# Reordering the start-up round of a fused RWKV-6 and MLP kernel: table load, row sums and two idle products

## The chip, the cores and the metric

The kernel runs on one core of a Trainium2 chip. The metric is the device time of one execution in microseconds (us), lower is better. Every run reported here gave the correct result. An execution is called fast when it is no more than 1.5% above the fastest of its kernel. All were, but for two: one of 22 executions of end_only, at 591.47 us (1.51% above), counts as slow and is left out of what follows, and one kernel was executed once, so its state is unknown. Here TensorE does the matrix products and transposes, VectorE, ScalarE and GpSimd work element by element, and SyncE issues most transfers (255 of 260 in the trace of the kernel before, ScalarE the other five).

## The reference

Two stages in fp32, with B=4, H=8, S=768, D=48, d_model=384, d_ff=1536:

```python
state = zeros(B, H, D, D)
for t in range(S):                                   # rwkv6_finch
    cur = einsum("bhd,bhe->bhde", u * k[t], v[t])
    y[t] = einsum("bhd,bhde->bhe", r[t], state + cur)
    state = w[t][..., None] * state + einsum("bhd,bhe->bhde", k[t], v[t])
x = y, heads side by side                            # (B, S, 384)
xn = (x - mean) / sqrt(var + 1e-6) * g_ln            # metaformer MLP
out = x + relu(xn @ w_ch1) @ w_ch2
```

## The kernel before

The work is cut into eight rounds, each of two units of four heads. A round transposes w, r and k, builds the lower triangle of the attention matrix in levels 0 to 5 (`quads` makes the products a_ps on TensorE, `grow` multiplies r and k by partial products of w on VectorE, `keep` puts the masked part into A), and forms states, outputs y and the MLP (h_ps, o_ps). The term of u needs only row sums of r·u·k: `product_sums`, called own_ps in the profile. Later rounds hide their attention under the MLP of the round before. Round 0 has no MLP to hide under, and all of the change lies there.

```python
def warm(n, tag="m"):              # idle products: only meant to keep TensorE's clock up
    while n > 0:
        m = min(n, RN // P)        # RN // P = 3, P = 128
        ps = (ps_m if tag == "m" else ps_t).tile([P, RN], F32, tag=tag, name="idle")
        PE.matmul(ps[:, 0 : m * P], nought.broadcast_to([P, P]),
                  nought.broadcast_to([P, m * P]), start=True, stop=True)
        n -= m

def product_sums(q):               # twelve products of TWO columns each
    ...
    for pr in pairs:
        for c in range(TT):
            PE.matmul(ps[:, ts(pr * TT + c, 2)], a["ruk"][pr][:, ts(c, P)],
                      sel[:, NP * g + pr], start=True, stop=True)
    ...
    ACT.copy(out=o.rearrange("p c (r j) -> p r c j", j=2),
             in_=ps[:, 0 : 2 * NK].rearrange("p (r c j) -> p r c j", r=NP, j=2))

def quads(q, lev):                 # 48 small products for one unit
    ...
    for c in range(NK):
        for i in range(2):
            for j in range(2):
                m = 2 * c + i
                rows = ds(HP * j, D)
                PE.matmul(a_ps[rnd][ds(C * (i ^ j), C), j, uu, c]...,
                          K[rows, ts(m, C)], R[rows, m, :, 1, :], start=True, stop=True)
```

The middle of round 0 (`run(ahead...)` makes six transposes for the next round; `begin` starts the load and conversion of a piece of the MLP's weights):

```python
for lev in range(1, NLEV):
    quads(u0, lev)
    quads(u1, lev)
    run(ahead[2 * lev - 2 : 2 * lev] if lev < NLEV - 1 else [])
    if lev in (2, 3, 4):
        begin()
    if lev == 1:
        product_sums(u0)
    elif lev < NLEV - 1:
        warm(3)
    for which in ("rk",) if lev < NLEV - 1 else "kr":
        for q in (u0, u1):
            grow(q, lev, which)
    keep(0, lev)
```

## Time and profile before

| | before |
|---|---|
| median of the first three runs | 587.24 us (587.1 to 587.42) |
| span of the profiled execution | 583.9 us |
| TensorE busy | 98% of the span |
| mean granted TensorE clock | 0.991 of full |

Two lines of the page of the kernel before also belong here. The first gives each engine's busy time, share and number of instructions (PE is TensorE, PEld its weight loads). The second gives, for one DMA queue, packets, megabytes and share of the sixteen DMA engines' time:

```profile
PE 572.2 (98%) x8558; PEld 384.1 (66%) x8558; DVE 273.6 (47%) x576; ACT 193.8 (33%) x423; POOL 90.6 (16%) x124
...
q8 instruction: 67, 1.10, 0.8%
```

TensorE executes 8558 products and as many weight loads, 17,116 instructions. Queue 8 carries 67 packets of 16.4 KB. Divided, that is 255 instructions for a packet, or 257 with the 92 waits of TensorE's sequencer. My estimate from these counts is that TensorE's program reaches it over this queue, in blocks of 256; shift64 below tests it. Over 584 us that is nothing, but in the levels of round 0 TensorE needs about 208 instructions in 2.9 us. The rate is the point there, not the share.

The chain of waits of the kernel before through levels 3, 4 and 5 of round 0 (start, length, what):

```profile
25.58 2.72 PE a_ps L49 x96
...
30.85 1.53 PE a_ps L49 x96
...
33.84 1.53 PE a_ps L49 x96
```

The products of level 3 run at half clock (2.72 in place of 1.53; the granted clock is 0.50 from 23.70 to 30.53), those of levels 4 and 5 at full clock. These three starts are what the change was to bring forward.

### The profile page before, as it was taken

How to read it: one execution, taken by the hardware profiler on the slowest of the kernel's cores; microseconds unless marked ns; L12 is line 12 of the kernel's file. 1: busy time of each engine (PE TensorE's matmuls, PEld its weight loads, DVE VectorE, ACT ScalarE, POOL GpSimd, SP SyncE). 2: the span in 40 equal slices, each digit the busy share in tenths (PEclk: the TensorE clock that was granted, in tenths of full speed). 3: DMA queues.
4: the chain of work that ended last, by engine and by line, in shares of the span. 5: the costliest groups of instructions: out<-in, count | busy, mean ns of one | idle time of the engine just before them, and what ended most of it. 6: DMA issues, size and time to landing. Idle time of an engine off the chain costs nothing.

```text
span 583.9 us, 19053 instructions
## 1 busy us (share of the span) xinstructions
PE 572.2 (98%) x8558; PEld 384.1 (66%) x8558; DVE 273.6 (47%) x576; ACT 193.8 (33%) x423; POOL 90.6 (16%) x124
## 2 busy tenths in 40 slices
PE   9999989999999999999999999999999999999997
PEld 7876756666666766666766666666666666666554
DVE  4879898687273634343452543336254531130000
ACT  3577686313442234311432125312331015202200
POOL 6140011104440035000620007000320000000000
PEclk9899899999999999999999999999999999999999
DMA  9938684036315311340204302031000000000000
GB/s 230 203 102 178 175 239 117 16 78 137 64 22 102 72 36 21 68 92 15 57 8 89 65 29 43 2 64 28 15 2 2 16 28 2 2 15 27 0 15 27
DMA packets 114192, 36.52 MB, mean 63 GB/s; under 512 B 104768, under 2 KB 111040, under 8 KB 114112
## 3 DMA queue, kind: packets, MB, share of 16 engines
q1 hardware_dynamic: 112240, 34.72, 26.5%
q8 instruction: 67, 1.10, 0.8%
q10 hardware_dynamic: 1872, 0.59, 0.4%
q14 instruction: 13, 0.11, 0.1%
HBM read 28.51 MB, written 4.72 MB: 57 GB/s over the span
## 4 chain that ended last, share of the span: by engine, by line
PE 91%; ACT 4%; DVE 2%; issue 1%; DMA 1%; ACTq 0%; DVEq 0%
PE o_ps L49 32%; PE h_ps L49 30%; PE a_ps L49 11%; PE y L49 4%; PE kv L49 2%; PE k_ps L49 2%; PE r_ps L49 2%; PE w_ps L49 2%; PE kn_ps L49 2%; PE xT_ps L49 1%; ACT rest L49 1%; PE own_ps L49 1%; PE idle L49 1%; ACT rkT L49 1%; ACT w_sb L49 1%
## 5 line engine op out<-in xcount | busy, mean ns | idle before, releaser
L49 PE MATMUL o_ps<-w_sb,h 128*128 128x384 f32 x576 | 199.0, 490 | 0.9 <-ACT h L49 0.9
L49 PE MATMUL h_ps<-xT,w_sb 128*128 128x384 f32 x576 | 198.7, 493 | 0.0
L49 PEld LDWEIGHTS h_ps<-xT,w_sb 128*128 128x128 f32 x576 | 105.7, 191 | 63.1 <-issue 0.9
L49 PEld LDWEIGHTS o_ps<-w_sb,h 128*128 128x128 f32 x576 | 104.4, 190 | 62.0 <-ACT h L49 1.8
L49 DVE TENSOR_TENSOR rkT<-rkT,tot 128x768 f32<-128x768 f32 (+1 forms) x96 | 76.7, 841 | 38.9 <-issue 26.0
L49 ACT ACTIVATE h<-h_ps 128x384 f32<-128x384 f32 x96 | 46.8, 488 | 144.7 <-PE h_ps L49 144.6
L49 PEld LDWEIGHTS a_ps<-rkT 48*64 48x64 f32 x4608 | 73.2, 136 | 20.8 <-issue 13.4
L49 PE MATMUL a_ps<-rkT 48*64 48x32 f32 x4608 | 78.4, 221 | 0.1
L49 DVE TENSOR_TENSOR o<-o_ps,x 128x384 f32<-128x384 f32 x24 | 13.4, 557 | 121.9 <-PE o_ps L49 121.8
L49 POOL TENSOR_TENSOR vo<-v,own 128x576 f32<-128x576 f32 x16 | 19.2, 1203 | 288.7 <-DVE own L49 251.9
L49 DVE SCALAR_TENSOR_TENSOR s<-s,decay,kv 128x48 f32<-128x48 f32 x160 | 29.3, 259 | 33.9 <-PE kv L49 33.9
L49 DVE TENSOR_TENSOR x<-y,vo 128x288 f32<-128x288 f32 x32 | 13.2, 453 | 53.8 <-PE y L49 53.7
L49 DVE COPY_PREDICATED A<-mask,a_ps 128x768 f32<-128x768 int8 x32 | 38.3, 1197 | 0.0
L49 ACT COPY rkT<-k_ps 128x384 f32<-128x384 f32 x31 | 13.9, 478 | 57.3 <-PE k_ps L49 57.1
L49 ACT ACTIVATE xT<-xT_ps,g_sb 128x384 f32<-128x384 f32 x24 | 13.6, 579 | 54.0 <-PE xT_ps L49 54.0
L49 ACT COPY rkT<-r_ps 128x384 f32<-128x384 f32 x31 | 14.2, 478 | 24.2 <-PE r_ps L49 24.1
L49 DVE TENSOR_SCALAR w_sb<-w_sb 128x384 f32<-128x384 f32 (+1 forms) x48 | 19.5, 406 | 0.8
L49 ACT ACTIVATE rstd<-mv,eps 128x3 f32<-128x3 f32 x8 | 2.4, 296 | 49.2 <-DVE mv L49 49.1
L49 DVE TENSOR_REDUCE own<-rk 128x12 f32<-128x576 f32 x12 | 9.0, 750 | 20.7 <-POOL rk L49 20.6
L49 ACT COPY wT<-w_ps 128x384 f32<-128x384 f32 x31 | 14.0, 478 | 14.1 <-PE w_ps L49 14.1
L49 PE MATMUL r_ps<-ident,nat_r 128*128 128x128 f32 x108 | 16.2, 279 | 2.2 <-ACT rkT L49 2.1
L49 DVE TENSOR_TENSOR rkT<-rkT,wT 128x768 f32<-128x768 f32 x16 | 17.5, 1131 | 0.9 <-PE a_ps L49 0.8
(76 smaller groups left out, 517.9 us busy)
## 6 DMA issues: line engine op xcount, KB each, us to landing
raw<-in_moe_w_ch_dram SPq DMA_DIRECT2D x24, 384.0 KB, 4.3
v<-in_v_dram SPq DMA_DIRECT2D x48, 96.0 KB, 3.3
out_dram<-o SPq DMA_DIRECT2D x24, 192.0 KB, 1.9
nat_w<-in_w_dram SPq DMA_DIRECT2D x42, 96.0 KB, 2.9
nat_r<-in_r_dram SPq DMA_DIRECT2D x42, 96.0 KB, 2.8
nat_k<-in_k_dram SPq DMA_DIRECT2D x42, 96.0 KB, 3.1
vx<-v SPq DMA_DIRECT2D x28, 72.0 KB, 2.3
nat_r<-in_r_dram ACTq DMA_DIRECT2D x2, 288.0 KB, 4.9
```

The lines of the kernel that those rows point to most:

```text
L49: return lambda *args, **kw: self.tc.keep_in_program_order(f(*args, **kw))
```

## The change

It has four parts. (1) **Table**: ScalarE loads its function table and takes its first root while nat_r is still in flight; the load of r of unit 1 goes later, and the load of g_sb goes to SyncE. (2) **Sums**: in level 1 the row sums of unit 0 go between the two halves of the products. (3) **Idle in level 1**: the idle product, so far in levels 2 to 4, is added there. (4) **End**: an idle product of three pieces before the outputs of unit 0 becomes one of two pieces before the outputs of unit 1.

```diff
--- before.py
+++ after.py
@@ -155,10 +155,17 @@
             )
 
 
+    nought = const.tile([P, 1], F32, name="nought")
+    DVE.memset(nought, 0.0)
+    eps = const.tile([P, 1], F32, name="eps")
+    DVE.memset(eps, 1e-6)
+    load_rows("r", 0, ACT)
+
+    ACT.activation(out=const.tile([P, 1], F32, name="root"), in_=eps, func=AF.Sqrt)
     for q in range(U):
         load_rows("w", q, SPO)
-        load_rows("r", q, ACT)
         load_rows("k", q, SPO)
+    load_rows("r", 1, ACT)
 
     sel = const.tile([P, H // 2, 2], F32, name="sel")
     POOL.memset(sel, 0.0)
@@ -167,16 +174,9 @@
             out=sel[ds(HP * j, D), :, j], in_=u.rearrange("(r j) d -> j d r", j=2)[j]
         )
     g_sb = const.tile([P, KC], F32, name="g_sb")
-    ACT.dma_start(out=g_sb, in_=moe_g_ln.rearrange("(kc p) -> p kc", p=P))
     u_bc = const.tile([P, H, D], F32, name="u_bc")
     ident = const.tile([P, P], F32, name="ident")
     make_identity(nc, ident)
-    nought = const.tile([P, 1], F32, name="nought")
-    DVE.memset(nought, 0.0)
-    eps = const.tile([P, 1], F32, name="eps")
-    DVE.memset(eps, 1e-6)
-
-    ACT.activation(out=const.tile([P, 1], F32, name="root"), in_=eps, func=AF.Sqrt)
     for q in range(U):
         for nm in "wrk":
             POOL.memset(flat(nm, q)[:, NH * TT * D :], 0.0)
@@ -752,19 +752,20 @@
     begin()
     begin()
     load(new[1], "k", SPO)
+    SPO.dma_start(out=g_sb, in_=moe_g_ln.rearrange("(kc p) -> p kc", p=P))
     warm(3)
     grow(u1, 0)
     keep(0, 0)
     ahead = each(turned, new[:1], "wrk", pairs) + each(turned, new[1:], "wrk", pairs)
     for lev in range(1, NLEV):
         quads(u0, lev)
+        if lev == 1:
+            product_sums(u0)
         quads(u1, lev)
         run(ahead[2 * lev - 2 : 2 * lev] if lev < NLEV - 1 else [])
         if lev in (2, 3, 4):
             begin()
-        if lev == 1:
-            product_sums(u0)
-        elif lev < NLEV - 1:
+        if lev < NLEV - 1:
             warm(3)
         for which in ("rk",) if lev < NLEV - 1 else "kr":
             for q in (u0, u1):
@@ -786,12 +787,12 @@
     product_sums(u1)
     own_term(u1, POOL)
     own_outputs(u0)
-    warm(3, "t")
     outputs(u0)
     exchanged(u1)
     begin()
     shifted()
     own_outputs(u1, "m")
+    warm(2, "t")
     outputs(u1)
     moments(0)
     load(units_of(2)[0], "w", SPO)
```

## The prediction

> **What bounds the kernel now.** I read the page first, then the chain of waits, then the timeline of single engines, then busy time and granted clock by stretch. The page says where a gain could lie at all:
>
> ```profile
> PE   9999989999999999999999999999999999999997
> PEclk9899899999999999999999999999999999999999
> PE 91%; ACT 4%; DVE 2%; issue 1%; DMA 1%; ACTq 0%; DVEq 0%
> ```
>
> TensorE is full in nearly all of the 40 slices of 14.6 us; all four parts of the change lie in the first 46 us of 583.9. The only slices where the granted clock falls below 9 tenths are the second and the fifth. So the change can save only what delays TensorE in the first three or four slices. Whatever is saved there is handed on, because the later rounds are an unbroken row of products.
>
> The chain of waits of the start (start, length, what):
>
> ```profile
> 0.80 4.04 DMA nat_r<-in_r_dram
> 4.86 0.39 ACTq L49
> 5.28 1.28 ACT L49
> 6.58 0.20 ACT root L49
> 6.78 0.38 ACT wT L49
> 7.20 1.53 PE r_ps L49 x12
> ```
>
> ScalarE issues its fifth transfer (g_sb) only when nat_r has landed (4.84), because that transfer reuses nat_r's completion semaphore; then come the function table (1.28), the root, and only then the copy that frees the bank for the transposes of r.
>
> The timeline of TensorE in level 1 and 2 of round 0 (start, length, product, count):
>
> ```profile
> 17.42 1.73 PE L49 MATMUL a_ps<-rkT 48*64 48x32 f32 x96
> 20.20 1.50 PE L49 MATMUL own_ps<-sel,ruk 128*128 128x2 f32 x12 [0.24 <-ACT wT L49]
> 24.09 1.49 PE L49 MATMUL idle<-nought 128*128 128x384 f32 x2
> 25.51 2.79 PE L49 MATMUL a_ps<-rkT 48*64 48x32 f32 x96
> ```
>
> The same 96 products take 1.73 us and then 2.79 us. Stretches of 3.41 us, TensorE alone, show why (stretch, length, busy and count, granted clock, DMA):
>
> ```profile
> 20.29:23.70 3.41, 3.41 (x113) 1.00 0.67 114
> 23.70:27.12 3.42, 3.42 (x66) 0.50 0.93 209
> 27.12:30.53 3.41, 3.41 (x53) 0.50 1.06 239
> 37.36:40.77 3.41, 3.41 (x137) 1.00 0.17 62
> 57.84:61.25 3.41, 3.41 (x94) 1.00 0.74 186
> 61.25:64.66 3.41, 3.41 (x9) 0.50 0.75 190
> ```
>
> The clock is halved from 23.70 to 30.53 and from 61.25 to 64.66. Every stretch before such a fall holds the sums (own_ps), 0.12 us each for two columns: TensorE counts as busy throughout, the array does almost nothing.
>
> [...] the edges 6.64, 23.70, 30.53, 61.25, 64.66 differ by 5, 2, 9 and 1 windows of 3.413. (Before 6.64 the page has no record and shows 1.00, but transposes start 0.213 us apart against 0.109 later, so it was half.) [...]
>
> To see what a window needs I estimate array work: a product of 384 columns on the whole array is two passes of 0.32 us (six passes take 1.94). Scaled by rows, columns and length, 96 pieces of a_ps make 0.48 us, six transposes 0.64, an idle product 0.64, twelve sums 0.02. The lowest shares of a window are then 0.10 (57.84, fell), 0.28 (20.29, fell), 0.36 (37.36, held). So a fall needs less than about 0.32. Cold windows with 0.61 and 0.64 stayed cold, 0.77, 0.82 and 0.84 became warm.
>
> **The change, part by part.**
>
> *Table first.* Table and root now run during nat_r's flight, at about 1.4 to 2.9. The second transfer of sel inherits the wait for nat_r (4.86 to about 5.4), in front of the first copy. w_ps_0 ends at 6.13, so that copy starts near 6.17, not 6.69. But the second half of w_ps, at half clock, ends at 7.10 anyway, and VectorE's copy of it runs 7.14 to 7.70: r_ps_0 can start at 6.94 instead of 7.20, r_ps_1 only at 7.75 instead of 7.91. A stall between groups costs one matmul's restart (0.06), and the chain then goes through VectorE's copies: 0.10 us remains of 0.52. nat_r of unit 1 leaves 1.6 us later, but its transposes come at 12.5: no cost. g_sb goes to SyncE and is used at 49.7: none.
>
> *Sums between the units.* Twelve sums, 1.42 us, move from behind w_ps to between the two halves (0.77 each) of the level's products. The 0.24 wait for a bank goes. The second half ends at about 20.3 instead of 19.0, so VectorE's second product of level 1 and its mask copy (1.87) end near 23.25 instead of 22.58.
>
> *Idle product in level 1.* Adds 0.75 (0.74 to 0.84 in the four warm cases). TensorE then reaches level 2 at 21.75 instead of 21.62, so the two parts cost 0.13 of TensorE in themselves. Their purpose is the clock. If no window fell, levels of 2.9 us (products 1.53, transposes 0.65, idle 0.75; VectorE needs 2.9 too) would bring level 5 to 30.65 instead of 33.77: 3.1 us saved.
>
> I don't believe all of that. With the window edges where this trace has them, 16.88 to 20.29 now holds the idle product, 96 pieces and the sums, but no longer the transposes: (0.32 + 0.48) / 3.41 = 0.24, which falls. The next, cold, holds transposes 1.28, idle 1.28 and some pieces, 0.84, and is warm again at 23.70. One cold window of 3.4 us in place of two: transposes +0.64, idle +0.53, pieces +0.35, so 1.5 of the 3.1 is given back, and 1.6 stays.
>
> *Idle at the end.* 384 columns between (0.84) become 256 at the new place (about 0.5): 0.35 saved. Nothing waits: sx of unit 0 is ready at 41.08 for a start at 41.4, sx of unit 1 at 43.06 for about 43.6.
>
> Sum: 0.10 + 1.6 + 0.35 = 2.05 us.
>
> **Rivals.**
>
> *The second fall.* Round 1's sums (24, 3.01 us) are untouched, but move against the windows. ScalarE waits 3.32 us for the h_ps behind them, so a cold window there is on the path; it costs h_ps 3.50 instead of 1.94. Shifted by about 1.7 to 2.2 us they straddle an edge (shares about 0.37 and 0.45) and the fall vanishes: total about 3.7. Shifted by 2.5, the fall comes in the middle of the sums and may last two windows: total about 0.5. Unshifted: 2.05.
>
> *No fall at all in round 0.* If the edges lie elsewhere, [...] all 3.1 may come, so 3.5 in all. For it: the idle product follows the sums closely. Against: my 0.24 and the 65% of positions that I count as falling.
>
> *The edges differ from execution to execution.* Then a kernel before without a fall is only 0.3 faster or so after, since the work itself shrinks by little. Against: three runs within 0.32 us.
>
> *VectorE takes over.* It is 4.9 of 5 us busy between 45 and 55, and 0.7 later in level 1. For a bound there: its mask copy. Against: it waited 1.54 us for cold products in level 3 and would catch up; worth 0.5 at most. A transfer as bound I exclude: weights are issued earlier, not later.
>
> **Range and chances.** The sum gives 2.05; I weigh it with 3.5 to 3.7 and with 0.3 to 0.5 about evenly on both sides and take 2.0: 587.24 - 2.0 = 585.2. The range goes from nearly everything (-3.9) to nearly nothing (-0.3): 583.3 to 586.9. Two per cent are 11.7 us, three times everything at stake, so "within 2%" is nearly sure.
>
> **What would show it.** The table load at about 1.4; the first copy of wT near 6.2 with r_ps starting near 6.95; level 5's products at 30.7 (no fall) to 32.2 (one window); the clock full at 23.7 to 27; y of unit 1 ending some 2 us before 44.77; the fall after round 1's sums gone or displaced. I am wrong in the mechanism if the clock still falls for two windows in round 0, and wrong about handing on if an early gain at 45 us is missing at 125.

## The result and the profile after

The changed kernel took 586.64 us (median of four runs, 586.47 to 587.8), the kernel before beside it 587.33 (four runs, 587.1 to 588.21). The ratio is 0.999, with a 95% interval of 0.9972 to 1.0007. A ratio here is the mean time of one kernel's fast runs over that of the other's of the same rounds, so not quite the ratio of the medians quoted. The gain of 2.0 us was not there. In the profiled executions the span even rose from 583.9 to 584.7.

The page of the kernel after, granted clock in 40 slices:

```profile
PEclk9979899999999999999999999999999999999999
```

The second slice of 14.6 us is clean now, but the third has 7 tenths: the fall of the clock in round 0 has moved, not gone.

The start on ScalarE, timeline of the kernel after (start, length, operation):

```profile
1.34 1.28 ACT L49 ACT_TABLE_LOAD   x1 [1.34 <-PEq L947]
...
5.59 0.48 ACT L49 COPY wT<-w_ps 128x384 f32<-128x384 f32 x1 [2.75 <-PE w_ps L49]
```

The table load starts at 1.34, as intended, and the first copy at 5.59 in place of 6.69. The chain of the kernel after has, at the place of the last line that the prediction shows of the start:

```profile
6.21 1.52 PE r_ps L49 x12
```

The transposes of r, at 7.20 before, start about 1.0 us earlier. The prediction gave 0.26 for their first and 0.10 for the chain, because it took the transposes of w to run at half clock. In this execution they ran at full clock (granted 1.00 from 4.34 on, where the trace before has this edge at 6.64), which the change did not bring about (see table_only below).

The chain of the kernel after through levels 3, 4 and 5. "Issue" is time in which TensorE waited for nothing that the profile shows:

```profile
27.78 1.53 PE a_ps L49 x96
...
30.11 1.37 issue
31.48 1.52 PE idle L49 x2
33.00 2.72 PE a_ps L49 x96
```

Here the whole case can be seen. Level 4's products start at 27.78, and before at 30.85: **3.07 us had been gained**, as much as the prediction thought possible for the clock. (Of these, 1.00 came with the early start: level 1's products begin at 16.49, and before at 17.49.) Then TensorE stands still for 1.37 us, the idle product runs at half clock, and level 5's products take 2.72 us. They start 0.84 earlier than before and end 0.35 later. The stretches show how the standstill and the clock belong together (stretch, length, TensorE's busy time and count, granted clock, DMA share, GB/s; kernel after):

```profile
28.23:31.64 3.41, 2.04 (x83) 1.00 1.12 226
31.65:35.06 3.41, 3.41 (x82) 0.50 0.71 212
35.06:38.47 3.41, 3.41 (x40) 0.50 0.04 13
```

TensorE is busy for only 2.04 of 3.41 us in the window that ends at 31.64; by the prediction's estimate of array work that is a share of about 0.30. For the next two windows the clock is halved. By 45 us the transposes of the next round start at 45.60 instead of 44.70: 3.07 us ahead has become 0.9 behind, and that is handed on to the end (+0.8 in the span).

What stood still at 30.11? The DMA view of the kernel after from 28.7 to 30.1 us, by queue (packets, MB, share of sixteen engines):

```profile
q1 hardware_dynamic: 1412, 0.26, 133.2%
q8 instruction: 1, 0.02, 5.0%
```

One packet of instructions is under way, among 1412 small data packets whose times add up to 133% of what sixteen engines have. It takes 0.05 × 16 × 1.4 = 1.1 us, landing at 29.97. TensorE goes on at 31.48. This became the theory called Supply below.

### The profile page after: what moved, and what is told of

Same layout as the page of the kernel before. It is cut to its first block, busy times and chain, and to the rows that moved or that the text cites. A ratio compares the mean times of both kernels' runs of the same rounds, so it can differ in the third digit from the quotient of the medians.

```text
span 584.7 us, 19058 instructions
## 1 busy us (share of the span) xinstructions
PE 571.7 (98%) x8560; PEld 383.3 (66%) x8560; DVE 273.5 (47%) x576; ACT 193.9 (33%) x423; POOL 91.5 (16%) x124
## 4 chain that ended last, share of the span: by engine, by line
PE 91%; ACT 4%; DVE 2%; issue 1%; POOL 1%; DVEq 0%; ACTq 0%; POOLq 0%
PE o_ps L49 32%; PE h_ps L49 30%; PE a_ps L49 11%; PE y L49 4%; PE kv L49 2%; PE k_ps L49 2%; PE w_ps L49 2%; PE kn_ps L49 2%; PE r_ps L49 2%; PE xT_ps L49 1%; ACT rest L49 1%; PE idle L49 1%; PE own_ps L49 1%; ACT rkT L49 1%; DVE w_sb L49 1%
```

## The experiments

Twelve kernels in three calls. Each call shares its runs of the kernel before: 59, 48 and 16 executions, with means of 587.19, 587.60 and 587.44 us.

### How they are read: cold windows

Each execution records its mean granted clock, and this explains most of the scatter. In the kernel before, the granted clock is 1.00 or 0.50, and its edges at 6.64, 23.70, 30.53, 61.25 and 64.66 us lie 5, 2, 9 and 1 times 3.413 us apart. Such a window of 3.413 us at a granted clock of 0.50 takes 3.413/2 off the full-speed time. So the number of **cold windows** in an execution is (1 − clock) × span / 1.706, rounded. (The cold start, ahead of the first edge, for which the traces have no record, isn't in it. In the kernel before, the transposes of w start 0.213 us apart ahead of that edge and 0.109 behind it.) For the 123 executions of the kernel before:

| cold windows | 0 | 1 | 2 | 3 | 4 | 5 | 6 |
|---|---|---|---|---|---|---|---|
| executions | 3 | 8 | 21 | 26 | 36 | 26 | 3 |
| mean us | 583.80 | 584.53 | 585.43 | 587.04 | 588.03 | 589.40 | 589.96 |

The same binary, on the same data, loses none to six windows, and its time runs from 583.14 to 590.89 us in step with that (correlation 0.93). I fitted all 279 fast executions of the three calls at once by least squares: time = a base for each call + a constant for each kernel + a cost for each cold window. **A cold window costs 1.14 ± 0.07 us** (± is two standard errors here and below). A kernel's constant is what it takes against the kernel before at an equal number of cold windows, if each costs the same wherever it falls.

| kernel | runs | mean us | ratio to before (95%) | cold windows, mean | constant, us |
|---|---|---|---|---|---|
| before | 123 | 587.19 / 587.60 / 587.44 | 1 | 3.34 / 3.46 / 3.56 | 0 |
| table_only | 22 | 586.83 | 0.9998 (0.9983 to 1.0012) | 3.45 | −0.49 ± 0.34 |
| level1_only | 14 | 588.28 | 1.0014 (0.9991 to 1.0037) | 3.21 | +1.23 ± 0.40 |
| end_only | 21 | 586.28 | 0.9981 (0.9960 to 1.0002) | 2.38 | +0.18 ± 0.35 |
| after_again | 14 | 586.99 | 0.9989 (0.9971 to 1.0008) | 3.29 | −0.15 ± 0.40 |
| before_wide | 22 | 584.56 | 0.9952 (0.9934 to 0.9970) | 0.32 | +0.54 ± 0.41 |
| after_wide | 15 | 584.08 | 0.9941 (0.9919 to 0.9962) | 0.27 | +0.12 ± 0.45 |
| after_wide_fill | 18 | 584.24 | 0.9933 (0.9914 to 0.9953) | 0.89 | −0.43 ± 0.41 |
| level1_wide | 6 | 584.06 | 0.9940 (0.9924 to 0.9956) | 0.00 | +0.68 ± 0.69 |
| table_end_wide | 6 | 583.77 | 0.9935 (0.9915 to 0.9955) | 0.17 | +0.20 ± 0.69 |
| after_wide_noidle | 6 | 583.72 | 0.9934 (0.9914 to 0.9955) | 0.33 | −0.04 ± 0.68 |
| after_wide_calm | 12 | 585.53 | 0.9963 (0.9942 to 0.9985) | 0.75 | +1.29 ± 0.55 |

Two theories were to be told apart. **Windows**: the clock's windows lie differently in each execution (the first edge at 6.64 us in the trace before, at 4.34 in the one after), so where one trace has its edges says nothing about the next, and the change gains only what it takes away in work. **Supply**: the gain of the early levels is lost to waiting for blocks of instructions. Their rival is the prediction's own account, in which the change turns two cold windows into one.

### First call: the parts alone, and the whole again

**after_again** is the changed kernel itself, for its spread and a second trace.

> The changed kernel once more, to narrow its gain. The first four runs gave 0.7 us of gain in the medians. Theory of instruction supply: gain between 0.3 and 1.2 us, and in this trace too TensorE pauses (over 0.3 us with all operands there) at the instruction numbers 256 apart of the first trace, whether or not the clock then falls. Rival (the pause of 1.37 us was an accident of that one execution): no pause there and a gain near 2 us.

It took 586.99 us on average against 587.19. Stretches of its trace (columns as above):

```profile
20.73:24.13 3.40, 3.40 (x36) 0.50 0.66 116
...
61.69:65.09 3.40, 3.40 (x12) 0.50 0.88 197
65.10:68.51 3.41, 3.41 (x11) 0.50 0.47 87
```

This execution has the one cold window after the level-1 sums that the prediction foresaw (20.73), where the first trace of the same kernel has none until 31.65. But another follows at 41.20 to 44.62, and the fall after round 1's sums lasts two windows. Over 14 executions the mean is 3.29 cold windows, and 3.34 for the kernel before in the same call: no fewer are seen, within ± 1.0. That fells the account in which two become one in every execution. Of the two standstills of the first trace this one has only that of level 3 (0.66 us), so what its expectation said of pauses came half true.

**table_only** keeps part 1 alone:

```diff
+    load_rows("r", 0, ACT)
+    ACT.activation(out=const.tile([P, 1], F32, name="root"), in_=eps, func=AF.Sqrt)
     for q in range(U):
         load_rows("w", q, SPO)
-        load_rows("r", q, ACT)
         load_rows("k", q, SPO)
+    load_rows("r", 1, ACT)
...   (nought and eps ahead of these, g_sb to SyncE, as in the change)
```

> Only the first part: table and root ahead of the other transfers, g_sb later. My prediction gave this part 0.10 us, because the half clock of the w transposes hid the rest. New theory: the gain depends on where the clock window lies at the start: about 0.1 us where the transposes of w run at half clock (r_ps then starts near 6.95), about 1.0 us where the clock is already full (r_ps near 6.1). On average 0.3 to 0.9 us faster than before. Rival (all hidden by the transfers of nat_w and nat_r): 0.0.

The mean is 0.4 ± 0.7 us below that of before, and 0.49 ± 0.34 at equal clock. In its trace the transposes of r start at 6.17. The 14 kept traces settle why. Each trace's clock record begins with an edge at 4.11 to 7.19 us, taken as the end of the cold start. With the table load moved (nine traces) the transposes of r start at 6.12 to 6.30 where that edge lies at 4.2 to 5.0, at 6.51 for an edge at 5.48, 6.96 for 6.61, and 7.18 and 7.22 for 7.07 and 7.19. With the load in its old place (five traces) they start at 7.20 to 7.40, wherever the edge is. Pairs with nearly the same edge give what the part saves at this place: 1.11 us (edges 4.11 and 4.23), 0.24 (6.64 and 6.61) and 0.18 (7.15 and 7.19). So what the part saves depends on where that edge lies, which the change doesn't set, and at the edge of the prediction's trace, 6.64, its 0.26 was right.

**level1_only** keeps parts 2 and 3 alone:

```diff
+        if lev == 1:
+            product_sums(u0)
         quads(u1, lev)
...
-        if lev == 1:
-            product_sums(u0)
-        elif lev < NLEV - 1:
+        if lev < NLEV - 1:
             warm(3)
```

> Only the second part: sums between the units' products and the idle product in level 1. My prediction: 1.6 us faster. New theory, instruction supply: TensorE's instructions come in blocks of 256, at 4.1 to 5.6 us a block in this stretch, so levels 1 to 5 of round 0 cannot get faster than that; what the full clock saves is given back as pauses at the ends of blocks (some 0.5 us in level 3 and 1.4 us near the end of level 4, at the same instruction numbers as in the changed kernel): 0 to 0.5 us faster. Rival (clock alone, no bound by supply): no such pauses, and 1.5 us or more faster.

The two parts that were to bring the whole gain made the kernel slower, if anything: by 1.1 ± 1.0 us (the ratio's interval holds 1), or 1.23 ± 0.40 at equal clock, with about as many cold windows (3.21). Neither theory had foreseen a loss. Its profiled execution fell for three windows, 19.54 to 29.78, right after the moved sums, and the pauses expected in levels 3 and 4 aren't in it.

**end_only** keeps part 4 alone:

```diff
     own_outputs(u0)
-    warm(3, "t")
     outputs(u0)
...
     own_outputs(u1, "m")
+    warm(2, "t")
     outputs(u1)
```

> Only the last part: idle product of 384 columns between becomes one of 256 behind the second unit's own products. My prediction: 0.35 us faster. New theory: 0.2 to 0.35, as y, idle and y follow one another without a wait; the rival (VectorE's additions set the pace there) gives 0.0.

Its 21 fast executions took 586.28 on average, with 2.38 cold windows, and +0.18 ± 0.35 at equal clock. So the 0.35 us of the prediction is not seen; the lower mean comes with fewer falls, which the 95% interval of the ratio does not separate from chance. Its trace is useful for another reason. The clock did not fall at all there, though the sums are those of the kernel before:

```profile
20.81:24.22 3.41, 3.41 (x114) 1.00 0.62 117
58.36:61.77 3.41, 3.41 (x24) 1.00 0.85 249
```

The first stretch is the window after level 1's sums, the second the one after round 1's. In the kernel before both places were at half clock. The parts sum to −0.49 + 1.23 + 0.18 = +0.9 ± 0.8, the whole is −0.15 ± 0.40. They do not add up, and why is not settled.

### Second call: the clock taken out, and the supply

**before_wide** and **after_wide** make each row sum write 64 columns instead of two. The instructions are the same in number and order, TensorE's time for twelve hardly changes (1.50 to 1.55 us in the trace), but the array has 32 times the columns to work on. The results are the same, since two of the columns are read.

```diff
-                ps[:, ts(pr * TT + c, 2)], a["ruk"][pr][:, ts(c, P)],
-                sel[:, NP * g + pr], start=True, stop=True,
+                ps[:, ts(pr * TT + c, 64)], a["ruk"][pr][:, ts(c, P)],
+                sel[:, NP * g + pr][:, None].broadcast_to([P, 32, 2]),
+                start=True, stop=True,
...
-            in_=ps[:, 0 : 2 * NK].rearrange("p (r c j) -> p r c j", r=NP, j=2),
+            in_=ps.rearrange("p (r c n) -> p r c n", r=NP, c=TT)[..., 0:2],
```

> The kernel before, with one thing changed: each of the sums' products streams 64 columns (the pair of selector columns repeated 32 times) instead of 2; as many instructions, the same weight loads, the same result. Theory (a window of 3.41 us falls when its array work, that is columns streamed times rows and columns of the array in use, is under about a third; sums do none): twelve sums then carry about 0.64 us of array work instead of 0.02, in the same 1.4 to 1.5 us, no clock falls in round 0 or behind round 1's sums, wherever the windows lie, and the mean drops from 587.2 to 583.3 to 584.8 us, with less spread than the 1.6 us of the kernel before. Rival (the clock falls by gaps in TensorE's busy time, or by the count of instructions): both are unchanged, so falls as before and 587 us.

> The changed kernel with the same 64 columns in the sums. With the clock full in every window, what is left of the change is its first and last part: 0.3 to 1.2 us faster than the kernel before with wide sums, that is a mean of 582.5 to 584.3 us. TensorE pauses at instruction numbers 961 and 1217 (counted over products and weight loads), 0.5 to 1.6 us each, since full speed runs ahead of the supply of instructions. Rival (level 1's new order gives 1.5 us or more of its own once the clock is full): 582 us or less.

Timeline at round 1's sums and the products behind them, first of the kernel before:

```profile
58.80 3.08 PE L49 MATMUL own_ps<-sel,ruk 128*128 128x2 f32 x24
61.74 3.63 PE L49 MATMUL h_ps<-xT,w_sb 128*128 128x384 f32 x6
```

and then of before_wide:

```profile
58.24 2.89 PE L49 MATMUL own_ps<-sel,ruk 128*128 128x64 f32 x24
...
60.97 2.15 PE L49 MATMUL h_ps<-xT,w_sb 128*128 128x384 f32 x6
```

and its stretches there:

```profile
57.28:60.69 3.41, 3.41 (x94) 1.00 0.71 160
60.69:64.10 3.41, 3.41 (x18) 1.00 0.93 224
```

TensorE is as fully busy as before, and now the clock stays up: the six h_ps behind the sums take 2.15 us, and 3.63 in the kernel before. Mean cold windows went from 3.46 to 0.32, and the time from 587.60 to 584.56. The terms agree: 0.54 − 1.14 × (3.46 − 0.32) = −3.0 us. That shows the cause of the falls behind the sums: it is their little work in the array, not any gap in TensorE's record. (Whether columns alone count, or columns times rows, the run doesn't separate.) Both wide kernels beat the kernel before of their call.

With the clock out of the way, what is the change worth? after_wide is 0.5 ± 0.7 us faster on average than before_wide (584.08 and 584.56; constants 0.12 and 0.54). That is about what the prediction had for its rival "the edges differ from execution to execution", 0.3. And the levels? Both traces have a mean clock of 1.000, so this is the prediction's case "no fall in round 0", in which level 5 was to start at 30.65. Timeline of before_wide, products of levels 3 and 5:

```profile
26.80 0.43 PE L49 MATMUL a_ps<-rkT 48*64 48x32 f32 x15 [0.58 <-issue]
...
31.86 1.60 PE L49 MATMUL a_ps<-rkT 48*64 48x32 f32 x96 [0.18 <-issue]
```

and the chain of after_wide:

```profile
26.30 0.51 issue
...
31.06 1.37 issue
32.43 0.91 PE idle L49 x2
33.35 1.53 PE a_ps L49 x96
```

With no fall in either, level 5 starts at 31.86 without the change and at 33.35 with it (33.28 in the timeline). Something other than the clock holds these levels, and it lets TensorE go on at the same time, 26.80, in both. Counting TensorE's records from 0 in the order of the trace (products, weight loads and waits of its sequencer) and setting them beside the packets of the instruction queue gives this (n is the number of the block's first instruction; pauses from start to start):

| kernel | block begun | at us | data of next block | next block begun | pause there |
|---|---|---|---|---|---|
| before | n=961 | 27.60 | 30.18 to 31.25 | 33.77 | 0.42 (not for the block) |
| after | n=705 | 21.77 | 23.53 to 24.41 | 25.84 | 0.75 |
| after | n=961 | 25.84 | 28.85 to 29.97 | 31.48 | 1.64 |
| before_wide | n=961 | 26.80 | 29.05 to 30.40 | 31.86 | 0.67 |
| after_wide | n=961 | 26.80 | 29.55 to 30.95 | 32.43 | 1.64 |

In these rows the transfer of a block starts 1.8 to 3.0 us after TensorE has begun the block before, while data loads fill the DMA engines (in the three rows of before and after, the packets of queue 1 add up to 87 to 101% of the sixteen engines' time meanwhile); it takes 0.9 to 1.4, and where TensorE paused for it the first instruction follows 1.43 to 1.51 later. Together that is 4.1 to 5.6 us for 256 instructions, where the level needs 208 in 2.9. (Later in the kernel a transfer starts up to 5.2 us before TensorE begins the block ahead of its own, as in the kernel after at 470.54 for 475.72, so lateness of this size is not seen throughout.) Over the 14 traces of this study there are 46 pauses of more than 0.45 us at a block's end, and in 45 of them the next instruction came 1.20 to 1.62 us after the data of its block had landed. So the account of levels that are bound by TensorE and VectorE alone was incomplete.

The table also says why the change's own levels came out later at full clock: the added idle product is four instructions, so the block that in before_wide ended just ahead of level 5's products ends in after_wide just ahead of level 4's idle product. Before the change that product is done during the wait for the next block; after it, it comes behind the wait. level1_wide, a run of the third call with these levels and no other part of the change, repeats it: next block begun at 32.41 after a pause of 1.64, level 5 at 33.25. In table_end_wide, at full clock and without the added product, level 5 starts at 32.02. By the block at n=1985 the two kernels of the table are within 0.23 us again (43.77 and 44.00), because after_wide waits less for the next blocks.

**shift64** moves all later instructions by 60 places, by putting 16 small idle products (64 instructions) into the start and taking out four instructions. If the pauses belong to places in the program, they move by 60; if they belong to block ends, they stay at the count.

```diff
-    warm(8)
+    warm(6)
+    small = ps_a.tile([P, 2, 512], F32, tag="a", name="small")
+    for i in range(16):
+        ...  # 48x64 weights of nought, 32 columns
```

> The changed kernel with 16 small products (64 instructions more) in place of the last 256 idle columns (4 instructions less) ahead of the first transposes: 60 instructions are inserted before everything else. Theory of supply in blocks of 256: pauses and the ends of blocks stay at the numbers 705, 961, 1217 of the whole count, so they come 60 instructions earlier in the program: the one that stood ahead of the idle product of level 4 now stands inside the products of level 4, and the pause near 116 us (number 4289) moves 60 instructions earlier too. Rival (the pause belongs to the instruction it stands before): it stays with the idle product of level 4, now at number 1277.

In one execution (587.91 us, state unknown) the instruction that had been number 360 was number 420, and 2029 became 2089. The pauses stayed at counts that leave 193 when divided by 256: 1217 (0.26), 1473 (0.80) and 1985 (0.92). None was at 1277, where the pause of level 4 would have been carried. The chain of shift64 shows the one at 1985, within y:

```profile
42.30 2.18 PE y L49 x131
44.48 0.70 issue
```

The 1.37 at level 4's idle is gone, but that alone proves little, as the clock was halved until 28.69 in this execution; the counts of the other pauses carry the test. One part of the expectation missed: no pause was seen at 4289 (0.01 us).

**after_wide_fill** puts longer idle products where TensorE would wait for its block: levels 1 to 4 get 3, 5, 6 and 3 pieces.

```diff
-            warm(3)
+            warm((3, 5, 6, 3)[lev - 1])
```

> As the run before, with two more idle products in level 2 (256 columns) and in level 3 (384). If the pauses are waits for instructions, this idle work runs in their place and costs nothing: within 0.4 us of the run before, pauses shorter by about the idle work added. Rival (TensorE waits there for something else, or there is no pause): 1.2 us slower.

Chain of after_wide_fill in levels 3 and 4:

```profile
25.94 0.40 issue
...
30.88 0.81 issue
```

The added products took 0.43 + 0.65 us, the pauses fell from 0.51 and 1.37 to 0.40 and 0.81, and the time is 584.24 against 584.08 (−0.55 ± 0.6 by the constants, but 0.89 cold windows in place of 0.27). In these two pauses 0.67 of the 1.08 us of added work took the place of waiting, and the whole did not cost what it takes. A third pause, at n=1985, grew from 0.75 to 1.21. That agrees with the supply; with the scatter of the runs it is no strong proof.

### Third call: which combination, and the supply again

> The kernel before with wide sums, and of the change the second part alone (sums between the units' products, idle product in level 1). With the clock full in any case, that part can only show what its order and its 0.75 us of idle work cost. My prediction gave 0.13 us as its own cost; the theory of instruction supply gives -0.2 to +0.4 us against the kernel before with wide sums (584.6), since levels 1 to 5 wait for instructions anyway. Rival (VectorE's later mask copy sets the pace): +0.6 us or more.

> The kernel before with wide sums and the first and last part of the change, without the second. Theory: all that the change is worth with a full clock is in these two, so the same as the changed kernel with wide sums (584.1) within 0.4 us, and 0.3 to 1.0 us faster than the kernel before with wide sums (584.6). Rival (the second part carries the gain): 584.6 or slower.

> The changed kernel with wide sums, without the idle product in level 1. Theory: its 0.75 us of TensorE only fills time that would be spent waiting for instructions later, so taking it away changes the mean by less than 0.4 us from 584.1, and pauses get longer. Rival (TensorE's work bounds levels 1 to 5): 0.7 us faster, 583.4.

**level1_wide** has parts 2 and 3 with wide sums, **table_end_wide** parts 1 and 4 with wide sums, and **after_wide_noidle** is after_wide with the idle product of level 1 taken out again:

```diff
-        if lev < NLEV - 1:
+        if 1 < lev < NLEV - 1:
             warm(3)
```

They took 584.06, 583.77 and 583.72 us on average, six executions each, and cannot be told from after_wide. With wide sums parts 2 and 3 are worth +0.14 ± 0.8 (0.68 − 0.54), where with narrow sums they cost 1.23 ± 0.40; I can't say whether the two really differ. The idle product of level 1, meant to hold the clock, shows no gain once the sums do: without it −0.4 ± 1.2 us, which holds both what was expected and the rival's −0.7. As expected, pauses grew in its trace (0.69 at n=705, 1.74 at n=961).

**after_wide_calm** moves three starts of weight loads and conversions (`begin`) from levels 2 to 4 to behind level 5, so that the blocks of instructions meet fewer data packets.

```diff
-        if lev in (2, 3, 4):
-            begin()
...
+    begin()
+    begin()
+    begin()
     load_vx(u0, POOL)
```

> The changed kernel with wide sums, with the three conversions of weights in levels 2 to 4 of round 0, and so the three loads of 384 KB that follow them, moved behind level 5. Theory: an instruction block comes late because its packets wait among the data packets of the same 16 engines[...]. With fewer loads between 22 and 34 us the start after the ends of blocks 705 and 961 comes down from 1.6 and 2.8 us to under 1.5 us, and the pause at 1217 from 1.64 us to under 0.8 us. The time: 0.5 to 1.5 us faster if nothing else is hurt; not faster if the later weights then hold up ScalarE at 60 to 90 us. Rival (supply has a fixed latency, whatever the loads): starts and pauses unchanged.

The wait for the start of the block's data after n=961 fell from 2.75 to 2.06 us, where under 1.5 was expected, and the pause at 1217 from 1.64 to 0.82, where under 0.8 was expected. After n=705 the wait rose, from 1.64 to 1.82, and the pause at 961 from 0.72 to 1.06: there the expectation missed. The time is 1.4 us longer, for a reason that the chain of after_wide_calm shows:

```profile
31.69 0.45 ACT w_sb L49
...
36.28 0.33 ACT kn L49
```

ScalarE now makes the conversions in one piece (31.69 to 36.28), in front of the copy of kn that TensorE needs. So as a trial of what delays the blocks it is undecided, one better and one worse. As a version it is worse.

**The best versions** are those with wide sums: after_wide, table_end_wide and after_wide_noidle, at 583.7 to 584.1 us, 0.6 to 0.7% faster than the kernel before by their ratios, and some 3 us below the changed one (586.99, in another call). level1_wide and after_wide_fill can't be told from them.

## Why the prediction was right or wrong

**The verdict.** The time, 586.64 us, lay in the range of 583.3 to 586.9, and "within 2%" was right. The reason given for 585.2 was not, and lying in the range was in part luck: its upper edge stood for "nearly nothing", and the 14 runs of after_again have their mean at 586.99, just above it. The prediction had named its own sign of a wrong mechanism, that the clock still falls for two windows in round 0; in the first trace it did (31.65 to 38.48). Of 2.05 us, 0.7 came in the first comparison and 0.2 ± 1.0 in the second (586.99 and 587.19).

**"One cold window of 3.4 us in place of two ... 1.6 stays": failed.** The step was read from the edges of one trace ("with the window edges where this trace has them"). Over 14 and 59 executions the means are 3.29 and 3.34 cold windows. The single cold window after level 1 is to be seen in one of the two traces of the changed kernel and not in the other, and a later fall came in its stead or besides it.

**The rival that was put aside fits best.** "The edges differ from execution to execution" was dismissed because "three runs within 0.32 us" spoke against it. Those three were close together by chance: 123 executions of that kernel span 7.8 us. With the falls removed the change is worth 0.5 ± 0.7, which fits the 0.3 of that rival and shuts out 2.0.

**"Levels of 2.9 us ... would bring level 5 to 30.65": failed.** In after_wide nothing fell, and level 5 started at 33.35 in the chain. The missing term is the supply of instructions, 5.6 us for the block that begins in level 3. The estimate counted TensorE's and VectorE's work and no time for the program to arrive; "a transfer as bound I exclude" looked at weights alone.

**"Whatever is saved there is handed on": failed inside round 0.** 3.07 us at level 4 became 0.9 the other way by 45 us. After that the sentence holds: of the 0.9, 0.8 is still there at the end.

**Sums and idle product "cost 0.13 of TensorE in themselves": too small.** From level 1's first product to level 2's it is 4.60 us in after_wide and level1_wide and 4.26 in before_wide, and 4.54 against 4.20 in the two kernels of the study: 0.34. Moving the sums saves 0.31 (3.95 in after_wide_noidle) and the idle product costs 0.65. The prediction's own terms, 0.75 added and a wait of 0.24 gone, don't make 0.13 either. The rest of the harm in level1_only (+1.23) came behind that.

**Table: the mechanism right, the size off.** The load came at 1.34 (1.4 predicted) and the first copy at 5.59 (6.2 predicted). The 0.10 assumed that the transposes of w stay at half clock, as they do in some traces and not in others (see table_only); the mean over 22 executions is 0.49 ± 0.34.

**Idle at the end, 0.35: not seen.** It is +0.18 ± 0.35 in end_only and −0.3 ± 0.8 in table_end_wide against before_wide, which also holds the table part. The term was too large in any case: at its new place the idle product takes 0.63 in the chains, not about 0.5, so at most 0.21 of 0.84 was to be had.

**The estimate of array work held.** Over the 14 profiles all 16 falls followed a window with a share of 0.32 or less, and of the windows that held one alone lay lower (0.29). The prediction had put the limit at about 0.32, and the wide sums follow from it: twelve sums of two columns were estimated at 0.02 us of array work in 1.5 us. Three of the seven wide traces still fell once (at 28.12, 36.20 and 45.97), after windows in which TensorE was busy for only 1.88 to 2.19 of 3.41 us: standing still lowers the share as well, so that waiting, for blocks of instructions among other things, seems to bring falls too. The second fall, after round 1's sums, lasted two windows in after_again and in shift64, as its rival foresaw, one in the first trace of the same changed kernel, and none in end_only: it too follows the execution, not the change.

**VectorE taking over: hardly.** Only in end_only and table_end_wide does the profile have level 5's products wait for its mask copy (0.73 us), and there they also start 1.48 and 1.50 us after their block's data landed, as they do where nothing but the block is missing.

## What to carry to other kernels

TensorE "busy" was not work in the array here: the stretches with the products of two columns looked full in the record (3.41 of 3.41 us) and were followed by a granted clock of 0.50, and making each of these products wider, at the same instruction count and nearly the same time, took the mean from 3.46 to 0.32 cold windows and brought 3 us, where moving them brought none. Before predicting from one trace's clock, count the cold windows in many executions; if their number scatters, predict the change of its mean and not the place of an edge. Where products are small, hold the number of instructions per microsecond against what the instruction queue delivers under the data traffic of that moment: here 256 in 4.1 to 5.6 us in the levels in which the loads were dense.
